# Tile 1's first h blocks, batch 1's second transposes and second x, and tile 1's PSUM banks placed anew in a fused attention and snake-MLP kernel

## The chip, the cores and the metric

The kernel runs on one core of one Trainium2 chip. Its time is device microseconds of one execution. Engines: PE (TensorE, matmuls), PEld (its weight loads), DVE (VectorE), ACT (ScalarE), POOL (GpSimd), SP (SyncE, which issues most DMAs).

## What is computed

Linear attention over 8 batches of 8 heads, 576 positions, 64 wide, then an MLP of width 512 -> 2048 -> 512 with a snake activation:

```python
def _attn_ref(q, k, v):
    q_s = exp(q - max(q, -1));  q_s = q_s / (sum(q_s, -1) + 1e-09)     # over the head's width
    k_s = exp(k - max(k, 2));   k_s = k_s / (sum(k_s, 2) + 1e-09)      # over the positions
    kv = np.einsum('bhsd,bhse->bhde', k_s, v)
    return np.einsum('bhsd,bhde->bhse', q_s, kv)

def _moe_ref(x, w_in, w_out, alpha):       # x: (4608, 512), the heads side by side
    h = x @ w_in
    s = np.sin(alpha * h)
    g = h + s * s / (alpha + 1e-09)
    return g @ w_out
```

## The kernel before

The 4608 positions make 8 batches for the attention and 9 tiles of 512 columns (`MF`) for the MLP. The program is a manual schedule: each engine runs its instructions in the order in which the Python code issues them, and waits at semaphores. So a line moved in the source moves work on every engine that it issues to.

Per batch, with the heads as two groups `ii` (0 and 1) of two pairs:

- `exp_half`, `exp_to` (L117): ACT takes exponentials of q and k, from fp32 stages filled by SP's DMAs, to bf16 `qe` and `ke`.
- `q1_sums`, `q1_norm` (L485 to L490): DVE sums and normalises q to `qn` for batch 1.
- `transpose_q1` (L472, with L199): eight PE transposes of one group into a PSUM tile `tp` of pool "a", copied by DVE to `qT` (L475).
- `cast_v1` (L467 to L470): v of batch 1 is cast to bf16 `vb`, places 0 to 4 of nine by ACT, 5 to 8 by POOL.
- `kv_mm` (L172): 36 small matmuls per group make k^T v, with the sums of k in one more column, in the PSUM tile `kvp` of pool `ps_k` (one buffer of two banks). `kv_norm` (L182, L183): DVE divides, to `kbd`.
- `x_half` (L477 to L481): `attn_x` (L216) multiplies `kbd` and `qT` in four matmuls into two banks; one bank is copied by ACT, the other by DVE, to two of the four 128-row chunks of `xT`, the MLP's input.

Per tile, with 16 blocks `ni` of 128 hidden units:

- `mm_h` (L254 to L262): four matmuls per block over the four chunks of `xT`, in the order `KO = (0, 2, 1, 3)`; chunks 0 and 2 come from group 0, 1 and 3 from group 1. `mm_h(t, ni, k0, k1)` does a part of the four; `h_slot` (L410) finishes a block that was begun.
- `sine` (L267): ACT's sine of the block, into one of four buffers `s`; the square is made by ACT (L269), POOL (L271) or DVE (L273), as the string `SQ` says for each block.
- `combine` (L277): DVE adds s*s/alpha and h, to `g`. With that the block's PSUM bank is free.
- `mm_o` (L281): 64 matmuls per tile of `g` with `w_out`; `evac_o` (L293, L296) copies the sums out and issues two output DMAs each on SP. `take(os, n)` issues the next n of a tile's `mm_o`.

PSUM has eight banks. In this stretch pools "a" and "b" have two each, "l" two, "k" (`ps_k`) two as one buffer. `BANKS` gives, for each tile, the pool of each of the 16 blocks; a pool hands out its buffers in turn, and the matmul that opens a buffer waits for the last reader of what lay there.

The change lies between tile 0's h blocks and tile 1's. There the code interleaves: the 64 `mm_o` of tile 0 (42, 10, 4, 4 and the last 4); batch 1's attention; then tile 1's 16 blocks. The parts stand in this order: norm and transposes of group 0; first kv (group 0); transposes of group 1; the loads of q's last place (`q8`) and of batch 2; cast of v's second group; first x; second kv; second x; exponentials of `q8`, and the sine table load (L525); tile 1's blocks (L554 to L557). `late_q8` uses `ps_k` again behind blocks 11 and 15. Then tile 1's `mm_o` start in the pools "o" and "p" (L561 on).

`load` and the `q8` loads are gated: a copy of one zero element by DVE (L514) stands ahead of a DMA into the same buffer, so that the DMA waits for it.

Of the kernel before, what the change touches and what calls it, by code (L numbers as in the profile page):

```python
# [15 lines left out]
F32 = mybir.dt.float32  # L16
# [7 lines left out]
def kernel(  # L24
# [23 lines left out]
    MF = 512  # L48
# [19 lines left out]
    xT = singles.tile([128, 4, NX], BF16, name="xT")  # L68
# [9 lines left out]
    def src_view(t, b):  # L78
        return t[b].rearrange("(i e) (p j) d -> (e p) i (j d)", e=2, j=J)
# [7 lines left out]
    def load(name, t, b, halves=False, eng=nc.sync, gate=None):  # L87

        st = stage.tile([128, 4, J, D], F32, name=f"st_{name}", tag="st")
        for ii in range(2) if gate else ():  # L90
            gate(st[:, ii, 0, 0:1], zero)
        view = src_view(t, b)
        flat = st.rearrange("p i j d -> p i (j d)")
        if halves:
            for ii in range(2):
                eng.dma_start(out=flat[:, ii::2], in_=view[:, ii::2])
        else:
            eng.dma_start(out=flat, in_=view)
        staged[name, b] = st

    def load_batch(b):
        load("q", q, b)
        load("k", k, b)
        load("v", v, b)
# [10 lines left out]
    def exp_to(dst, src, iis=range(2)):  # L115
        for ii in iis:
            nc.scalar.activation(dst[:, :, ii * 128:(ii + 1) * 128].rearrange("p j (x d) -> p x j d", x=2),  # L117
                                 src[:, ii::2], AX.Exp)
# [43 lines left out]
    def kv_mm(b, ii, pool, split=False):  # L162

        if ii == 0 or split:
            A["kvp", b] = pool.tile([128, 2, 512], F32, name="kvp", tag="a")
        kvp, ke, vt = A["kvp", b], A["ke", b], vb[b % 2]
        for j in range(J):
            for x in range(2):
                h = 2 * ii + x
                for e in range(2):  # L170
                    r = slice(64 * e, 64 * e + 64)
                    nc.tensor.matmul(kvp[64 * x:64 * x + 64, e, ii * 65:(ii + 1) * 65],  # L172
                                     ke[r, j, h * 64:(h + 1) * 64],
                                     vt[r, j, h * 65:(h + 1) * 65],
                                     start=(j == 0), stop=(j == J - 1))

    def kv_norm(b, i0=0, i1=2):

        kt, m = kbd[b % 2], i1 - i0
        kvr = small.tile([128, 2, 2], F32, name="kvr")[:, :, 0:m]  # L180
        src = A["kvp", b][:, :, i0 * 65:i1 * 65].rearrange("p e (ii c) -> p e ii c", ii=m)
        nc.vector.reciprocal(kvr, src[:, :, :, D])  # L182
        nc.vector.tensor_tensor(kt[:, :, i0:i1], src[:, :, :, 0:D],  # L183
                                kvr.unsqueeze(3).to_broadcast([128, 2, m, D]), op=ALU.mult)

    def q_tile(b):
        if ("qT", b) not in A:
            A["qT", b] = att2.tile([128, 2, J, 128], BF16, name="qT")
        return A["qT", b]
# [6 lines left out]
    def q_transpose_ii(b, ii, j0, j1, tp):  # L196

        for j in range(j0, j1):
            nc.tensor.transpose(tp[:, j - j0], A["qn", b][:, ii, j], identb)  # L199
# [11 lines left out]
    def attn_x(b, ii, j0, j1, outs):  # L211

        for e in range(2):
            for x in range(2):
                r = slice(64 * x, 64 * x + 64)
                nc.tensor.matmul(outs[x][64 * e:64 * e + 64], kbd[b % 2][r, e, ii],  # L216
                                 A["qT", b][r, ii, j0:j1, e * 64:(e + 1) * 64], start=True, stop=True)
# [24 lines left out]
    G = {}  # L242

    HP = {}
    BANKS = {0: "aabbkllaabbkllaa", 1: "kbbllaakbbllaabb", 2: "aabbopaabbopaabb"}

    def bank(kind):

        if kind == "k":
            return ps_k.tile([128, 2, MF], F32, name="kvp", tag="a")[:, 0]  # L250
        pool = {"a": lambda: ps_h[0], "b": lambda: ps_h[1], "l": lambda: ps_l, "o": lambda: ps_o[0], "p": lambda: ps_o[1]}[kind]()
        return pool.tile([128, MF], F32, name={"l": "lp", "o": "op", "p": "op"}.get(kind, "hp"), tag=kind)

    def mm_h(t, ni, k0=0, k1=4):  # L254

        if ni == 0 and k0 == 0:
            G[t] = gpool.tile([128, nN, MF], BF16, name="g")
        hp = HP[t, ni] if k0 else bank(BANKS.get(t, 3 * "aabb" + "abba")[ni])
        HP[t, ni] = hp
        for k in range(k0, k1):  # L260
            nc.tensor.matmul(hp, win[:, KO[k], ni * 128:(ni + 1) * 128],  # L261
                             xT[:, KO[k], t * MF % NX:t * MF % NX + MF], start=(k == 0), stop=(k == 3))  # L262
        return hp

    def sine(t, ni, hp, sq):
        s = spool.tile([128, MF], F32, name="s")
        nc.scalar.activation(s, hp, AX.Sin, scale=alpha_sb[:, ni:ni + 1])  # L267
        if sq == "A":
            nc.scalar.activation(s, s, AX.Square)  # L269
        elif sq == "P":  # L270
            nc.gpsimd.tensor_tensor(s, s, s, op=ALU.mult)  # L271
        else:
            nc.vector.tensor_tensor(s, s, s, op=ALU.mult)  # L273
        return s
# [25 lines left out]
    ACT_CP, DVE_CP, GP_CP = nc.scalar.copy, nc.vector.tensor_copy, nc.gpsimd.tensor_copy  # L300
# [21 lines left out]
    ps_k = ES.enter_context(tc.tile_pool(name="ps_k", bufs=1, space=PSUM, reuse_waits="tile"))  # L322
# [70 lines left out]
    xp = [bank("b") for _ in range(2)]  # L393
# [8 lines left out]
    xp = [bank("l") for _ in range(2)]  # L402
# [5 lines left out]
        mm_h(0, ni, ki, ki + 1)  # L408

    def h_slot(t, ni, sq, lag):  # L410
        hp = mm_h(t, ni, 2 if ni < (4, 1, 0)[min(t, 2)] else 0)
        lag.append((t, ni, hp, sine(t, ni, hp, sq)))

    def flush(lag, keep):
# [3 lines left out]
    def o_quad(t, accs, engs):  # L418

        R = range(4)  # L420
        by_m, by_n = [(n, m) for m in R for n in R], [(n, m) for n in R for m in R]
        orders = [by_m, by_n, by_n, by_n[:8] + [(n, m) for m in R for n in (2, 3)]]
        for c in R:
            for n, m in orders[c]:
                mm_o(t, m, 4 * c + n, accs[m])
                if c == 3 and n == 3:
                    evac_o(t, m, accs[m], engs[m])
                yield

    def take(it, n=1000):  # L430
        for _ in range(n):
            if next(it, 0) == 0:
                return
# [4 lines left out]
    with ES:  # L438
# [26 lines left out]
        os = o_quad(0, accs, [DVE_CP, ACT_CP, DVE_CP, DVE_CP])  # L465

        def cast_v1(ii):  # L467
            vv = vb[1].rearrange("p j (i c) -> p i j c", i=4)
            for j0, j1, eng in ((0, 5, ACT_CP), (5, 9, GP_CP)):
                eng(vv[:, 2 * ii:2 * ii + 2, j0:j1, 0:D], staged["v", 1][:, ii::2, j0:j1])  # L470

        def transpose_q1(ii, eng):  # L472
            tp = ps_h[0].tile([128, 8, 128], BF16, name="tp", tag="a")
            q_transpose_ii(1, ii, 0, 8, tp)
            eng(q_tile(1)[:, ii, 0:8], tp)  # L475

        def x_half(ii):  # L477
            xp = [bank("a") for _ in range(2)]
            attn_x(1, ii, 0, 8, xp)
            for x in range(2):  # L480
                (ACT_CP, DVE_CP)[x](xT[:, 2 * x + ii, MF:2 * MF], xp[x])  # L481

        def q1_sums(ii):
            part, src = qs1[:, :, 2 * ii:2 * ii + 2], qe1[:, ii]
# [3 lines left out]
        def q1_norm(ii):  # L488
            part = qs1[:, :, 2 * ii:2 * ii + 2]
            nc.vector.tensor_tensor(A["qn", 1][:, ii, 0:8].rearrange("p j (x d) -> p j x d", x=2), qe1[:, ii],  # L490
                                    part.unsqueeze(3).to_broadcast([128, 8, 2, D]), op=ALU.mult)
# [15 lines left out]
        exp_half("k", 1, 1)  # L507
        q1_norm(1)
        take(os, 10)
        kv_mm(1, 0, ps_k, split=True)  # L510
        kv_norm(1, 0, 1)
        transpose_q1(1, DVE_CP)
        for b in range(2):
            DVE_CP(q8[:, 0, b, 0:1], zero)  # L514
            nc.sync.dma_start(out=q8[:, :, b], in_=src_view(q, b)[:, :, 8 * D:J * D])
        load_batch(2)
        cast_v1(1)
        take(os, 4)
        x_half(0)
        kv_mm(1, 1, ps_k, split=True)  # L520
        kv_norm(1, 1, 2)
        take(os, 4)
        x_half(1)
        exp_to(A["qe", 1][:, J - 2:J], q8)
        nc.scalar.activation(zero, zero, AX.Sin)  # L525
        take(os)
        for ki in range(2):
            mm_h(1, 0, ki, ki + 1)
        norm_q8()
        load("q", q, 3)  # L530
        load("k", k, 3)
# [33 lines left out]
    def o_stream(t, eng=DVE_CP):  # L565
        for j in range(4):
            acc = bank("op"[j % 2])
            for ni in range(nN):
                mm_o(t, j, ni, acc)
                if ni == nN - 1:  # L570
                    evac_o(t, j, acc, eng)
                yield
# [4 lines left out]
    os = o_stream(1)  # L577
# [14 lines left out]
    for ii in range(2):  # L592
        xp = [bank("ab"[ii]) for _ in range(2)]
# [29 lines left out]
    for ni in range(nN):  # L623
# [4 lines left out]
        elif ni in (9, 13):  # L628
            ii = ni // 12
# [3 lines left out]
    for t in range(3, nT):  # L633
        b = t + 1 if t + 1 < B else None
        os = o_stream(t - 1)
# [9 lines left out]
        for ni in range(nN):  # L645
            hp = mm_h(t, ni)
# [62 lines left out]
```

## Time and profile before

| | |
|---|---|
| median of 3 runs | 283.23 us (282.95 to 283.6) |
| the profiled execution | 282.79 us, of it 281.0 us span of the profile |
| PE busy | 267.7 us (95%), 1890 matmuls |
| ACT busy | 223.8 us (80%) |
| DVE busy | 185.5 us (66%) |
| POOL busy | 81.3 us (29%) |
| granted PE clock | 9 tenths or more in every slice |
| DMA | 45.82 MB, mean 163 GB/s |

The span is what the profile sees, from the first instruction to the last. A time line shows start and length in us from the span's start, the engine, the line of the kernel, the operation, what it writes and reads, its shape, and in brackets the idle time of the engine just ahead of it with what ended that. Lengths overlap where an engine pipelines: matmuls above all, whose modelled end lies some 0.16 us behind the next one's start. The chain of waits follows the work that ended last back to what released it at each step. Some matmul records are missing from a trace, so a group of four can read x3.

### The profile page before, as it was taken

The page shows a single profiled execution, that of the slowest core. Times are in us where ns is not written, and L with a number is a line of the kernel's source. Part 1 is how long each engine was busy: PE and PEld are TensorE (multiplying, and loading weights), DVE is VectorE, ACT ScalarE, POOL GpSimd, SP SyncE. Part 2 cuts the span into 40 slices and gives each one's busy share as a digit, 9 for nine tenths or more (in the row PEclk, how much of TensorE's full clock was granted, in tenths as well). Part 3 has the DMA queues.
Part 4 walks back from the last instruction along what each step waited for, and adds up shares of the span by engine and source line. Part 5 has one row for each costly group of instructions (what it writes and reads, how often), then busy time and mean ns, then how long its engine had stood idle before and what let it go on. Part 6 is the DMA issues. An engine that isn't in the chain of part 4 may idle for free.

```text
span 281.0 us, 4925 instructions
## 1 busy us (share of the span) xinstructions
PE 267.7 (95%) x1890; PEld 124.0 (44%) x1919; DVE 185.5 (66%) x279; ACT 223.8 (80%) x322; POOL 81.3 (29%) x77
## 2 busy tenths in 40 slices
PE   2899989999999999999999999999999999999994
PEld 1444444444443444444444444444444444444443
DVE  3968776899878767766776677577775555555412
ACT  5899458999588999899989998999877777777400
POOL 2968121777667460205003500350000000000000
PEclk9999999999999999999999999999999999999999
DMA  7999999997599039712991199125011111111143
GB/s 263 299 194 232 278 307 319 361 343 253 120 229 399 2 81 334 290 37 48 267 383 45 37 263 392 38 50 124 8 29 40 37 37 37 40 41 42 40 106 75
DMA packets 39320, 45.82 MB, mean 163 GB/s; under 512 B 17008, under 2 KB 22656, under 8 KB 39296
## 3 DMA queue, kind: packets, MB, share of 16 engines
q1 hardware_dynamic: 33392, 40.58, 46.9%
q0 software_dynamic: 5744, 4.79, 10.3%
q8 instruction: 15, 0.25, 0.3%
q10 hardware_dynamic: 160, 0.13, 0.2%
q14 instruction: 9, 0.07, 0.1%
HBM read 36.71 MB, written 9.44 MB: 164 GB/s over the span
## 4 chain that ended last, share of the span: by engine, by line
PE 85%; DMA 8%; POOL 2%; issue 1%; SPq 1%; ACT 1%; DVE 1%; ACTq 0%
PE op L281 38%; PE hp L261 38%; DMA st_v<-in_v_dram 4%; DMA win<-in_moe_w_in_dram 2%; PE lp L261 2%; PE kvp L172 2%; DMA st_k<-in_k_dram 2%; PE op L261 1%; PE op L679 1%; POOL s L271 1%; PE kvp L261 1%; PE hp L216 1%; PE xp L216 1%; POOL st_v L306 1%; DVE g L277 1%
## 5 line engine op out<-in xcount | busy, mean ns | idle before, releaser
L277 DVE SCALAR_TENSOR_TENSOR g<-s,inva_sb,hp 128x512 bf16<-128x512 f32 x128 | 94.5, 746 | 58.7 <-ACT s L269 53.3
L261 PE MATMUL hp<-xT,win 128*128 128x512 bf16 x506 | 127.7, 379 | 0.6 <-PE lp L216 0.2
L281 PE MATMUL op<-wout,g 128*128 128x512 bf16 x478 | 121.0, 379 | 1.6 <-issue 1.1
L267 ACT ACTIVATE s<-hp,alpha_sb 128x512 f32<-128x512 f32 x128 | 86.1, 682 | 22.3 <-PE hp L261 21.0
L261 PEld LDWEIGHTS <-win 128*128 128x128 bf16 x576 | 55.7, 98 | 67.8 <-DMA win<-in_moe_w_in_dram 1.2
L281 PEld LDWEIGHTS <-g 128*128 128x128 bf16 x560 | 53.4, 98 | 64.8 <-issue 2.3
L269 ACT ACTIVATE s<-s 128x512 f32<-128x512 f32 x112 | 70.5, 630 | 3.5
L271 POOL TENSOR_TENSOR s<-s 128x512 f32<-128x512 f32 x29 | 30.1, 1053 | 17.6 <-ACT s L267 11.3
L151 POOL TENSOR_TENSOR qn<-qe,qs 128x1152 bf16<-128x1152 bf16 x11 | 23.2, 2127 | 29.5 <-DVE qs L145 24.4
L293 DVE COPY o<-op 128x512 f32<-128x512 f32 (+2 forms) x33 | 21.8, 661 | 10.2 <-PE op L281 7.9
L136 POOL CAST vb<-st_v 128x1152 bf16<-128x1152 f32 x12 | 14.7, 1257 | 45.6 <-DMA st_v<-in_v_dram 45.6
L117 ACT ACTIVATE qe<-st_q 128x1152 bf16<-128x1152 f32 (+2 forms) x18 | 17.7, 1025 | 6.1 <-DMA st_q<-in_q_dram 6.0
L117 ACT ACTIVATE ke<-st_k 128x1152 bf16<-128x1152 f32 x16 | 17.9, 1151 | 3.2 <-DMA st_k<-in_k_dram 3.2
L144 DVE TENSOR_REDUCE qs<-qe 128x36 f32<-128x2304 bf16 x5 | 12.8, 2551 | 8.3 <-ACT qe L117 8.3
L117 ACT ACT_TABLE_LOAD x7 | 9.0, 1283 | 0.8 <-PEq L693 0.7
L172 PE MATMUL kvp<-vb,ke 64*64 64x65 bf16 x576 | 6.9, 194 | 2.2 <-ACT vb L470 1.5
L349 PE MATMUL warm<-qe,identb 128*128 128x512 bf16 x10 | 4.1, 554 | 5.0 <-ACT qe L117 5.0
L281 PE MATMUL hp<-wout,g 128*128 128x512 bf16 x31 | 8.6, 379 | 0.1
L172 PEld LDWEIGHTS <-ke 64*64 64x64 bf16 x576 | 6.0, 106 | 6.1 <-issue 3.4
L281 PE MATMUL lp<-wout,g 128*128 128x512 bf16 x30 | 8.4, 379 | 0.2 <-issue 0.2
L261 PE MATMUL lp<-xT,win 128*128 128x512 bf16 x30 | 7.5, 379 | 0.1
L229 DVE CAST xT<-xp 128x1024 bf16<-128x1024 f32 (+1 forms) x7 | 7.4, 1065 | 0.0
(89 smaller groups left out, 135.8 us busy)
## 6 DMA issues: line engine op xcount, KB each, us to landing
out_dram<-o SPq DMA_DIRECT2D x70, 128.0 KB, 2.4
st_q<-in_q_dram SPq DMA_DIRECT2D x6, 1152.0 KB, 6.3
st_k<-in_k_dram SPq DMA_DIRECT2D x6, 1152.0 KB, 8.6
st_v<-in_v_dram SPq DMA_DIRECT2D x6, 1152.0 KB, 11.3
st_k<-in_k_dram SPq DMA_DIRECT2D x4, 576.0 KB, 8.1
st_q<-in_q_dram SPq DMA_DIRECT2D x4, 512.0 KB, 6.0
st_v<-in_v_dram SPq DMA_DIRECT2D x3, 576.0 KB, 10.0
wout<-in_moe_w_out_dram POOLq DMA_DIRECT2D x3, 512.0 KB, 12.7
```

The lines of the kernel that those rows point to most:

```text
L117: nc.scalar.activation(dst[:, :, ii * 128:(ii + 1) * 128].rearrange("p j (x d) -> p x j d", x=2), src[:, ii::2], AX.Exp)
L136: engs[ii](vv[:, 2 * ii:2 * ii + 2, :, 0:D], staged["v", b][:, ii::2])
L144: nc.vector.tensor_reduce(qs, A["qe", b].rearrange("p j (i d) -> p j i d", i=4), axis=AXL.X, op=ALU.add)
L151: engs[ii % len(engs)].tensor_tensor(qn[:, ii, 0:j1].rearrange("p j (x d) -> p j x d", x=2), qe[:, ii], part.unsqueeze(3).to_broadcast([12 ...
L172: nc.tensor.matmul(kvp[64 * x:64 * x + 64, e, ii * 65:(ii + 1) * 65], ke[r, j, h * 64:(h + 1) * 64], vt[r, j, h * 65:(h + 1) * 65], start= ...
L261: nc.tensor.matmul(hp, win[:, KO[k], ni * 128:(ni + 1) * 128], xT[:, KO[k], t * MF % NX:t * MF % NX + MF], start=(k == 0), stop=(k == 3))
L267: nc.scalar.activation(s, hp, AX.Sin, scale=alpha_sb[:, ni:ni + 1])
L269: nc.scalar.activation(s, s, AX.Square)
L271: nc.gpsimd.tensor_tensor(s, s, s, op=ALU.mult)
L277: nc.vector.scalar_tensor_tensor(G[t][:, ni], in0=s, scalar=inva_sb[:, ni:ni + 1], in1=hp, op0=ALU.mult, op1=ALU.add)
L281: nc.tensor.matmul(acc, G[t][:, ni, j * 128:(j + 1) * 128], wout[:, ni, :], start=(ni == 0), stop=(ni == nN - 1))
L293: eng(o[:, cols], acc)
```

## The change

- `BANKS[1]` is "aabbllkaabblaabb" in place of "kbbllaakbbllaabb".
- `h_slot` of tile 1 finishes two begun blocks (0 and 1), where it was one (0).
- `transpose_q1(1)` stands ahead of `kv_mm(1, 0)` and `kv_norm`, where it stood behind them.
- `cast_v1(1)`: the places 0 to 4 are cast by DVE, where it was ACT; it stands behind the first x, where it stood ahead of it.
- `x_half` takes its banks as an argument, and for group 0 ACT and DVE change places in the copies. Group 1's two banks are one tile of `ps_k`.
- The first two of the four matmuls of tile 1's blocks 0 and 1 stand between the first x and the second kv. Before, those of block 0 alone stood behind the last `mm_o` of tile 0.

```diff
-    BANKS = {0: "aabbkllaabbkllaa", 1: "kbbllaakbbllaabb", 2: "aabbopaabbopaabb"}
+    BANKS = {0: "aabbkllaabbkllaa", 1: "aabbllkaabblaabb", 2: "aabbopaabbopaabb"}
...
-        hp = mm_h(t, ni, 2 if ni < (4, 1, 0)[min(t, 2)] else 0)
+        hp = mm_h(t, ni, 2 if ni < (4, 2, 0)[min(t, 2)] else 0)
...
-            for j0, j1, eng in ((0, 5, ACT_CP), (5, 9, GP_CP)):
+            for j0, j1, eng in ((0, 5, (ACT_CP, DVE_CP)[ii]), (5, 9, GP_CP)):
...
-        def x_half(ii):
-            xp = [bank("a") for _ in range(2)]
+        def x_half(ii, xp):
             attn_x(1, ii, 0, 8, xp)
             for x in range(2):
-                (ACT_CP, DVE_CP)[x](xT[:, 2 * x + ii, MF:2 * MF], xp[x])
+                (ACT_CP, DVE_CP)[x ^ 1 ^ ii](xT[:, 2 * x + ii, MF:2 * MF], xp[x])
...
         take(os, 10)
+        transpose_q1(1, DVE_CP)
         kv_mm(1, 0, ps_k, split=True)
         kv_norm(1, 0, 1)
-        transpose_q1(1, DVE_CP)
...
         load_batch(2)
+        take(os, 4)
+        x_half(0, [bank("a") for _ in range(2)])
         cast_v1(1)
-        take(os, 4)
-        x_half(0)
+        for ki in range(2):
+            for ni in range(2):
+                mm_h(1, ni, ki, ki + 1)
         kv_mm(1, 1, ps_k, split=True)
         kv_norm(1, 1, 2)
         take(os, 4)
-        x_half(1)
+        xb = ps_k.tile([128, 2, MF], F32, name="kvp", tag="a")
+        x_half(1, [xb[:, x] for x in range(2)])
...
         take(os)
-        for ki in range(2):
-            mm_h(1, 0, ki, ki + 1)
```

## The prediction

> **What bounds the kernel now.** I read the page first (PE busy 95% of the span, granted clock full in every slice), then the waits of PE: after 59 us it waits for no other engine to the end of the span (1.1 us of "issue" in seven pieces is all that is listed). So whatever moves the moment at which tile 1's out matmuls (L281, first at 59.7 us) begin, moves the end by the same amount; only the stretch from 36 to 60 us has to be worked out. The chain of waits there:
>
> ```profile
> 29.41 12.43 DMA st_v<-in_v_dram
> 41.86 0.75 ACT vb L470
> 42.65 0.48 PE kvp L172 x32
> 43.13 1.00 PE hp L281 x4
> ...
> 45.44 0.86 PE kvp L261 x4
> ```
>
> Batch 1's second half of v lands at 41.84, ACT casts it, and only then PE's second kv product runs; from there the chain is PE alone. PE's time line (start, length, instruction, idle time before it):
>
> ```profile
> 41.00 0.41 PE L216 MATMUL hp<-qT,kbd 64*64 64x512 bf16 x4
> 42.65 0.48 PE L172 MATMUL kvp<-vb,ke 64*64 64x65 bf16 x36 [1.24 <-ACT vb L470]
> 43.11 1.02 PE L281 MATMUL hp<-wout,g 128*128 128x512 bf16 x4
> 44.06 0.41 PE L216 MATMUL hp<-qT,kbd 64*64 64x512 bf16 x4
> 44.63 0.81 PE L281 MATMUL lp<-wout,g 128*128 128x512 bf16 x3 [0.16 <-issue]
> 45.28 1.03 PE L261 MATMUL kvp<-xT,win 128*128 128x512 bf16 x4
> ...
> 55.92 3.62 PE L261 MATMUL hp<-xT,win 128*128 128x512 bf16 x16
> ```
>
> The hole of 1.24 us ahead of the second kv is all there is to gain. Blocks 12 to 15 of tile 1 are the last row. A 128x512 matmul takes a slot of 0.216 us (L261's rows: 45.28 to 46.14 for four). ACT:
>
> ```profile
> 40.49 1.16 ACT L117 ACTIVATE ke<-st_k 128x1152 bf16<-128x1152 f32 x1 [1.36 <-DMA st_k<-in_k_dram]
> 41.86 0.74 ACT L470 CAST vb<-st_v 128x640 bf16<-128x640 f32 x1 [0.21 <-DMA st_v<-in_v_dram]
> 42.50 0.57 ACT L481 CAST xT<-hp 128x512 bf16<-128x512 f32 x1
> 44.17 0.58 ACT L293 COPY o<-hp 128x512 f32<-128x512 f32 x1 [1.10 <-PE hp L281]
> 44.65 0.59 ACT L481 CAST xT<-hp 128x512 bf16<-128x512 f32 x1
> 47.29 0.67 ACT L267 ACTIVATE s<-kvp,alpha_sb 128x512 f32<-128x512 f32 x1
> ```
>
> After its last copy of x, ACT has a fixed road to tile 1's first sine: from 44.65 to 47.29, 2.64 us (two exponentials, a table load). From 47.29 to 56.5 ACT never waits for PE. DVE at the end of that stretch:
>
> ```profile
> 55.84 0.75 DVE L277 SCALAR_TENSOR_TENSOR g<-s,inva_sb,hp 128x512 bf16<-128x512 f32 x1 [0.20 <-POOL s L271]
> 56.51 0.85 DVE L273 TENSOR_TENSOR s<-s 128x512 f32<-128x512 f32 x1
> 57.27 0.73 DVE L277 SCALAR_TENSOR_TENSOR g<-s,inva_sb,hp 128x512 bf16<-128x512 f32 x1
> ```
>
> These are block 8's combine, the square of block 10, block 9's combine: a PSUM bank comes free when its combine ends, block 8's at 56.59, block 9's at 58.01.
>
> **The change, part by part.** Clock times are those of the profiled run, so shifts can be read off.
>
> *Transposes ahead of the first kv (L199, L172).* PE is free at 38.80 (last L281 starts at 38.58), DVE's second norm ends at 38.67. Eight transposes take 0.44 (39.59 to about 40.04 before), kv follows at about 39.33 (0.09 for the change of tile size, as in the profile between L281 and L216) and ends at 39.8, 0.15 later than before. DVE now copies the transposes ahead of the norm of kv: 39.44 to 40.13, then 0.17 + 0.29 to about 40.55. The four L281 end at 40.61, the first x (L216) starts at 40.70 instead of 41.00. Worth 0.3 us to the copies of x, but ACT is busy with ke until 41.65 either way.
>
> *v's cast moved from ACT to DVE (L470), copies of x swapped.* ACT loses 0.74 us and its wait for v: its copy of x runs 41.55 to 42.13 instead of 42.50 to 43.07. DVE's copy of x runs 41.19 to 41.88, then the cast. The trace has the same shape on DVE once, in the start: 128x640, 0.62 us. With POOL casting its share at that moment (41.89, 0.62) the far bound is the trace's worst stretch of a POOL square, 1.49 beside a median near 1.04: 0.72 x 1.43 = 1.03, so v is ready between 42.5 and 42.95. I take 42.6; PE needs it at 43.13, so the cast costs nothing, with 0.2 us of cover even at the far bound.
>
> [...]
>
> *Blocks 0 and 1 begun behind the first x (L261).* Two mm_h of two k each, four matmuls, wait for ACT's copy: 42.18 to 43.04. Before, only two such (block 0) ran, later. The second kv starts at 43.04 + 0.09 = 43.13 instead of 42.65: **+0.48**. Everything behind it follows in the old order and spacing (kv to the first L261: 45.28 - 42.65 = 2.63): the second x at 44.54, ACT's evacuation (L293) and last copy of x +0.48, the remaining L261 from 45.76. There 60 of 64 matmuls are left; before, 60 were left at 46.14. So PE alone would be **0.38 ahead**.
>
> *Second x in kv's banks.* Both halves now lie in one tile, and in the changed kernel as built DVE's copy of the second half waits for ACT's copy of the first, which was not so before (DVE's began at 44.55, ACT's at 44.65, side by side). ACT's ends at 45.24 + 0.48 = 45.72, DVE's (0.69, L481) runs to 46.45, and block 0's last k waits until 46.50. Behind DVE's copy stand two evacuations and q8's norm, which ends near 49.2, before the first combine at 49.6. Before, the sixth L261 began at 45.28 + 5 x 0.216 = 46.36: PE is now **0.14 behind**.
>
> *Banks rotated.* Blocks 12 to 15 now take the banks of blocks 7 to 10 (distance 5). Before, the distances there were 7, 7, 6, 6. Block 14 waited for block 8's combine (56.59) and began at 55.92 + 8 x 0.216 = 57.65. Now it waits for block 9's, 58.01 in the old run: 0.41 us late (with 0.05 for the semaphore) even if ACT were not late at all. But the sines start 0.48 later (47.77), and since ACT runs without a wait for PE from there, every combine up to block 9 shifts by the same 0.48. Block 12 waits until 55.64 + 0.53 = 56.17 (0.10 behind PE's own 56.06), block 13 until 57.12, block 14 until 58.01 + 0.53 = 58.54: **+0.89**. Block 15 (block 10's combine, 58.67 + 0.48) is free in time. PE's 0.14 is inside that stall, not added to it. The out matmuls then follow 0.89 late; the last combine (62.89, shifted some 0.5, by sine 15 at about 60.9) is ready before its matmul at 62.95 + 0.89.
>
> *Queues.* q8's two loads hang on two DVE copies of one element, now at 40.55 instead of 40.85. SP's next three loads (batch 2) follow 0.3 us earlier. Nobody waits for them before 45.1 (q8) and 62 (batch 2). At worst they take 0.3 us from v's landing, and 42.6 + 0.3 is still before 43.13. Two ACT casts less and one DVE cast more: no other engine waits for these.
>
> **Sum.** PE is +0.48 at the second kv, -0.38 where the L261 resume, +0.14 at block 0's end, +0.89 from block 14 on. After that PE has no stall in which to lose it. The profiled run took 282.79 (span 281.0 and 1.8 around it), so its counterpart would take 283.68. The median of the runs is 283.23, so I predict 283.23 + 0.89 = **284.1 us**; by the bounds of the switch before the second kv (0 or 0.09) and of the cast, 283.9 to 284.3.
>
> **Rivals.**
> B: the ring does not bind, only DVE's wait for ACT counts: +0.14, 283.4. It would need ACT's sines to catch up 0.75 us before block 9. Against it: ACT's only slack there is about 0.1 us (52.74 to 52.76 and the like).
> C, the other side: the hole is filled and nothing given back: -0.38, 282.85. Its place is the L261 resuming at 45.76; it decides if DVE's copy does not really wait for ACT's and combine 9 ends before 57.3, that is 0.7 us earlier than in the old run. For it: ACT sheds 0.74 us. Against: that is shed ahead of the x copy, and spent again waiting for the later kv.
> D: more is lost. If the profiled run's v landed early, or casts and squares slow each other like the 1.49 us POOL row, combine 9 slips by another 0.45: +1.3, 284.5.
> The reverse also weakens the forecast: where v lands later in other runs, before pays for it and after does not, until 0.5 us; with 0.3 of that the loss is 0.6.
>
> **Numbers.** Chances: forecast 0.62, B 0.13, C 0.12, D 0.13. About 0.2% (0.57 us) is what a measurement tells from no change: the forecast and D are beyond it but for the case of a late v (0.04); B and most of C are within; a part of C, with luck in the runs, is beyond on the fast side. So slower 0.71, same 0.20, faster 0.09. The range reaches from between C and B to above D: 283.0 to 284.7.
>
> **What would show it.** In the new profile: the first x near 40.7; four L261 near 42.2 with the hole gone; the second kv near 43.1; DVE's copy from kvp starting as ACT's ends, near 45.75, with PE idle about half a us; the first sine near 47.8; PE idle ahead of block 14, released by DVE L277, the out matmuls at 60.6. Wrong if the first sine starts before 47.3 or the copies run side by side.

## The result, and the profile after

| | before | after |
|---|---|---|
| median of 22 runs each | 282.61 us (281.86 to 284.51) | 283.87 us (283.61 to 285.43) |
| the profiled execution | 282.79 us, span 281.0 | 283.86 us, span 282.1 |
| second kv (L172) starts | 42.65 | 43.15 |
| tile 1's first sine (L267) starts | 47.29 | 47.75 |
| block 14 (L261) starts | 57.65 (worked out: 55.92 + 8 x 0.216) | 58.74 |
| first out matmul (L281) starts | 59.71 | 60.81 |

The ratio is 1.0043, with a 95% interval of 1.0032 to 1.0053: the change makes the kernel slower by 1.26 us. The two profiled executions differ by 1.07 us, and the first out matmul by 1.10. From 59 us on PE waits for no other engine; all that is listed there is "issue", 1.1 us in seven pieces, as before:

```profile
PE op L281 <- issue: 1.1, 7, 0.2
PE hp L261 <- DVE g L277: 0.4, 1, 0.4
```

(Waits of PE in the kernel after, from 59 us to the end: total, times, longest, in us. The second line is the wait that ended at 58.74, ahead of the row that reaches into this stretch.) So the loss lies whole between 40 and 61 us. PE's time line there (start, length, instruction, idle time before it):

```profile
40.98 0.41 PE L216 MATMUL hp<-qT,kbd 64*64 64x512 bf16 x4
42.18 1.04 PE L261 MATMUL hp<-xT,win 128*128 128x512 bf16 x4 [0.79 <-DVE xT L480]
43.15 0.48 PE L172 MATMUL kvp<-vb,ke 64*64 64x65 bf16 x36
45.76 0.38 PE L261 MATMUL hp<-xT,win 128*128 128x512 bf16 x1
46.49 2.53 PE L261 MATMUL hp<-xT,win 128*128 128x512 bf16 x11 [0.35 <-DVE xT L480]
...
56.16 2.18 PE L261 MATMUL hp<-xT,win 128*128 128x512 bf16 x8
58.74 1.89 PE L261 MATMUL hp<-xT,win 128*128 128x512 bf16 x8 [0.40 <-DVE g L277]
```

The hole of 1.24 us that the kernel before had ahead of the second kv is gone. In its place stand 0.79 ahead of the four early matmuls, 0.35 inside block 0, 0.40 ahead of block 14, and one that no bracket shows: blocks 12 and 13 (56.16) take 2.18 where eight matmuls take 1.89, so 0.29 is idle ahead of block 13. Starts with the same work left tell it best: against the kernel before, PE is 46.49 - 46.36 = 0.13 behind at the sixth L261, 56.16 - 55.92 = 0.24 at block 12, 1.09 at block 14. Nearly all of the loss arises in the last stretch of the tile.

ACT, DVE and POOL show why. ACT:

```profile
44.63 0.59 ACT L293 COPY o<-hp 128x512 f32<-128x512 f32 x1 [2.58 <-PE hp L281]
45.12 0.59 ACT L480 CAST xT<-kvp 128x512 bf16<-128x512 f32 x1
47.75 1.25 ACT L267 ACTIVATE s<-hp,alpha_sb 128x512 f32<-128x512 f32 x2
...
50.96 1.35 ACT L267 ACTIVATE s<-lp,alpha_sb 128x512 f32<-128x512 f32 x2
```

DVE (four of its rows; L158 and L159, a reduction and a reciprocal of q8's norm, end just ahead of L160):

```profile
42.04 0.71 DVE L470 CAST vb<-st_v 128x640 bf16<-128x640 f32 x1
45.74 0.69 DVE L480 CAST xT<-kvp 128x512 bf16<-128x512 f32 x1 [0.85 <-ACT xT L480]
48.49 0.69 DVE L160 TENSOR_TENSOR qe<-qe,qs 128x512 bf16<-128x512 bf16 x1
50.12 2.06 DVE L277 SCALAR_TENSOR_TENSOR g<-s,inva_sb,hp 128x512 bf16<-128x512 f32 x3 [0.93 <-POOL s L271]
```

ACT idles 2.58 us, because what it copies out (L293) hangs on the later kv; its copy of x starts at 45.12, DVE's only as that ends. POOL:

```profile
41.78 0.62 POOL L470 CAST vb<-st_v 128x512 bf16<-128x512 f32 x1 [2.38 <-DMA st_v<-in_v_dram]
48.51 1.58 POOL L271 TENSOR_TENSOR s<-s 128x512 f32<-128x512 f32 x1 [6.10 <-DVE qs L159]
```

The first square of the tile takes 1.58 us, where the same instruction took 1.03 in the kernel before:

```profile
48.04 1.03 POOL L271 TENSOR_TENSOR s<-s 128x512 f32<-128x512 f32 x1 [5.53 <-DVE qe L160]
```

In the kernel after it starts 0.02 us behind DVE's product L160 and ends at 50.09; the first combine follows at 50.12. From there, by the code and the times, the delay goes on over the four buffers `s`: sine 4 writes the buffer that block 0's combine has to have read. That combine ends at 50.12 + 0.75 = 50.87, and sine 4 starts at 50.96 (the profile names no releaser for so short a wait), 3.21 behind the first sine. (In the kernel with q8's norm moved ahead, told below, it is 2.95.) Every later sine, square and combine stands behind that.

The chain of waits ahead of block 14 leads through four instructions:

```profile
55.44 1.05 POOL s L271
56.49 0.03 issue
56.52 0.75 DVE g L277
57.27 0.76 DVE s L273
58.03 0.67 DVE g L277
58.70 0.04 issue
```

Block 8's square, block 8's combine, block 10's square, block 9's combine: then block 9's bank is free, and block 14 opens it. That is the ring of banks with its new distance of 5. Block 9's combine starts at 57.95, where it started at 57.27 before. Of these 0.68 us, 0.46 is the later first sine, and 0.22 was added behind it.

### The profile page after: what moved, and what is told of

Its sections match the earlier page's. It is cut to its first block, busy times and chain, and to the rows that moved or that the text cites. A ratio compares the mean times of both kernels' runs of the same rounds, so it can differ in the third digit from the quotient of the medians.

```text
span 282.1 us, 4926 instructions
## 1 busy us (share of the span) xinstructions
PE 268.0 (95%) x1890; PEld 123.8 (44%) x1919; DVE 186.1 (66%) x280; ACT 223.7 (79%) x321; POOL 82.0 (29%) x77
## 4 chain that ended last, share of the span: by engine, by line
PE 88%; DMA 5%; POOL 2%; issue 1%; DVE 1%; ACT 1%; SPq 0%; ACTq 0%
PE op L281 38%; PE hp L261 37%; DMA win<-in_moe_w_in_dram 3%; PE hp L281 3%; PE lp L281 2%; PE kvp L172 2%; DMA st_k<-in_k_dram 2%; PE lp L261 2%; PE op L261 1%; PE op L680 1%; POOL win L107 1%; PE hp L216 1%; ACT s L267 1%; PE xp L216 1%; PE kvp L261 1%
## 5 line engine op out<-in xcount | busy, mean ns | idle before, releaser
L277 DVE SCALAR_TENSOR_TENSOR g<-s,inva_sb,hp 128x512 bf16<-128x512 f32 x130 | 95.8, 745 | 59.7 <-ACT s L269 53.3
L261 PE MATMUL hp<-xT,win 128*128 128x512 bf16 x514 | 129.7, 379 | 2.2 <-DVE xT L480 1.1
L281 PE MATMUL op<-wout,g 128*128 128x512 bf16 x478 | 121.0, 379 | 1.6 <-issue 1.1
L267 ACT ACTIVATE s<-hp,alpha_sb 128x512 f32<-128x512 f32 x130 | 87.5, 684 | 22.3 <-PE hp L261 20.6
L261 PEld LDWEIGHTS <-win 128*128 128x128 bf16 x576 | 55.8, 98 | 70.3 <-issue 2.4
L281 PEld LDWEIGHTS <-g 128*128 128x128 bf16 x560 | 53.4, 98 | 64.6 <-issue 2.1
L271 POOL TENSOR_TENSOR s<-s 128x512 f32<-128x512 f32 x29 | 30.7, 1073 | 18.2 <-ACT s L267 12.1
L293 DVE COPY o<-op 128x512 f32<-128x512 f32 (+2 forms) x33 | 21.8, 660 | 10.5 <-PE op L281 8.3
L281 PE MATMUL hp<-wout,g 128*128 128x512 bf16 x30 | 8.6, 379 | 0.3 <-issue 0.2
L281 PE MATMUL lp<-wout,g 128*128 128x512 bf16 x31 | 8.7, 379 | 0.0
L172 PEld LDWEIGHTS <-ke 64*64 64x64 bf16 x576 | 5.8, 106 | 4.8 <-issue 2.6
L172 PE MATMUL kvp<-vb,ke 64*64 64x65 bf16 x576 | 6.9, 194 | 1.0 <-ACT vb L331 0.6
L229 DVE CAST xT<-xp 128x1024 bf16<-128x1024 f32 (+1 forms) x7 | 7.4, 1065 | 0.0
L261 PE MATMUL lp<-xT,win 128*128 128x512 bf16 x26 | 6.8, 379 | 0.4 <-DMA win<-in_moe_w_in_dram 0.3
```

The costliest lines, as they stand in the source:

```text
L277: nc.vector.scalar_tensor_tensor(G[t][:, ni], in0=s, scalar=inva_sb[:, ni:ni + 1], in1=hp, op0=ALU.mult, op1=ALU.add)
L281: nc.tensor.matmul(acc, G[t][:, ni, j * 128:(j + 1) * 128], wout[:, ni, :], start=(ni == 0), stop=(ni == nN - 1))
L293: eng(o[:, cols], acc)
```

## The experiments

In all of them "before" is the kernel before, run on the same chip in the same comparison; times are medians. A stretch is read as the same two marks in each trace: "kv to out" is from the second kv's start to the first out matmul (17.06 us before, 17.66 after). Starts with a star are worked out from a longer row with 0.216 us a matmul.

| kernel | second kv | first sine | block 14 | first out | time minus before |
|---|---|---|---|---|---|
| before | 42.65 | 47.29 | 57.65* | 59.71 | |
| after | 43.15 | 47.75 | 58.74 | 60.81 | +1.26 |
| ring widened in after | 43.06 | 47.67 | 57.78* | 60.30 | +0.71 |
| new ring in before | 42.39 | 47.00 | 57.78 | 59.85 | +0.31 |
| no early blocks | 42.94 | 47.54 | 58.52 | 60.59 | +0.88 |
| q8's norm earlier | 43.28 | 47.88 | 58.65 | 60.72 | +1.15 |
| one copy on DVE | 43.22 | 47.33 | 58.20 | 60.27 | +0.85 |

**The ring alone, both ways.** In the kernel after, the last blocks get banks with longer distances; block 14 takes block 8's again (distance 6), as before the change:

```diff
-    BANKS = {... 1: "aabbllkaabblaabb", ...}
+    BANKS = {... 1: "aabbllkaabllbaab", ...}
```

> The changed kernel with tile 1's banks as aabbllkaabllbaab: blocks 12 to 15 reuse the banks of blocks 3, 7, 8, 9 (distances 9, 6, 6, 6) instead of 7, 8, 9, 10 (all 5). Ring theory: block 14 waits for block 8's combine (57.3 in the changed kernel's trace) and not block 9's (58.6), so PE's 0.40 us of idle ahead of block 14 goes; the first out matmul moves from 60.8 to about 60.4, where it now waits for block 11's combine (its bank is the one of block 11), so some 0.4 us less than the changed kernel, +0.8 over before. Rival, the DVE copy's wait for ACT is the loss: nothing changes, +1.2 over before.

Measured: 283.33 against 282.62, ratio 1.0029 (1.0019 to 1.0040). PE (two rows of its time line):

```profile
56.05 3.63 PE L261 MATMUL hp<-xT,win 128*128 128x512 bf16 x16
60.30 1.89 PE L281 MATMUL op<-wout,g 128*128 128x512 bf16 x8 [0.34 <-DVE g L277]
```

Blocks 12 to 15 run through without a stall. Almost half of the loss is gone (+0.71 in place of +1.26), though a new wait of 0.34 stands ahead of the out matmuls: it ends with block 11's combine, since the bank that the first of them opens was now block 11's. The reverse, the new string in the kernel before and nothing else:

```diff
-    BANKS = {... 1: "kbbllaakbbllaabb", ...}
+    BANKS = {... 1: "aabbllkaabblaabb", ...}
```

> The kernel before with nothing but the changed bank string of tile 1. Ring theory: block 14 waits for block 9's combine, 58.01 in the trace of before, and starts at 58.06 instead of 57.65: +0.41 us over before, PE idle just ahead of block 14, released by the combine. Rival, the rotation is harmless by itself: 0.0.

Measured: 282.93 against 282.62, ratio 1.0008 (0.9995 to 1.0020). By time alone this is no difference that the runs can tell; the trace shows the mechanism all the same:

```profile
55.59 1.89 PE L261 MATMUL hp<-xT,win 128*128 128x512 bf16 x8
57.78 1.89 PE L261 MATMUL hp<-xT,win 128*128 128x512 bf16 x8 [0.30 <-DVE g L277]
```

Block 14 could start at 55.59 + 8 x 0.216 = 57.32 and starts at 57.78. So the ring costs 0.46 us with the old timing of the sines, where 0.41 was reckoned. In both kernels with the new string block 14 waits for block 9's combine (0.30 and 0.40).

**The early blocks.** The four early matmuls go back behind the last out matmuls:

```diff
-        for ki in range(2):
-            for ni in range(2):
-                mm_h(1, ni, ki, ki + 1)
         kv_mm(1, 1, ps_k, split=True)
...
         take(os)
+        for ki in range(2):
+            for ni in range(2):
+                mm_h(1, ni, ki, ki + 1)
         norm_q8()
```

> The changed kernel with the four early matmuls of blocks 0 and 1 put back behind the last matmuls of tile 0's output, all else as changed. Theory (ACT's late start, handed on by the ring, sets the end): the second kv starts when DVE's cast of v is done, about 42.8 instead of 43.15, ACT's first sine at 47.4 instead of 47.75, block 14 and the end 0.35 us earlier than in the changed kernel, +0.85 over before, although PE loses the four matmuls in the hole. Rival, PE's own order is the bound (filling the hole is worth 0.86 less the 0.35 of the earlier kv): 0.5 us slower than the changed kernel, +1.7 over before.

Measured: 283.50 against 282.62, ratio 1.0035 (1.0020 to 1.0049).

```profile
42.94 0.48 PE L172 MATMUL kvp<-vb,ke 64*64 64x65 bf16 x36 [1.50 <-DVE vb L470]
...
58.52 1.89 PE L261 MATMUL hp<-xT,win 128*128 128x512 bf16 x8 [0.40 <-DVE g L277]
```

The kv comes only 0.21 earlier, not 0.48, because now v's cast on DVE holds it. Block 14 still waits 0.40, and it comes as much earlier (0.22) as the sines (0.21). So the end follows ACT and the ring, not the amount of work that PE has done ahead: the early blocks' lead, 0.38 by the prediction, is worth nothing here.

**DVE's wait for ACT.** The two banks of the second x are copied by DVE in one instruction, which takes the copy off ACT:

```diff
-        x_half(1, [xb[:, x] for x in range(2)])
+        attn_x(1, 1, 0, 8, [xb[:, x] for x in range(2)])
+        DVE_CP(xT[:, 1::2, MF:2 * MF], xb)
```

> The changed kernel with both halves of the second x copied by one DVE instruction (1.07 us, as the 128x1024 casts elsewhere), so DVE does not wait for ACT, and ACT is rid of its copy. Theory (ACT's first sine, handed on by the ring, sets the end): ACT's road starts 0.47 us earlier, first sine near 47.3, and block 14 starts 10.8 to 11.0 behind it as in the changed kernel and in the two runs with its ring (47.75 to 58.74; 47.54 to 58.52; 47.00 to 57.78): near 58.1 to 58.25, the end 0.5 to 0.65 earlier, +0.6 to +0.75 over before. Rival, PE's own order sets it: block 0's last k at 46.3 instead of 46.5, the end 0.2 earlier, +1.0 over before.

Measured: 283.44 against 282.59, ratio 1.0027 (1.0015 to 1.0038). The copy takes 1.23 us (not 1.07: the 128x1024 casts elsewhere in these traces, L229, take 1.22 too), almost as long as the two in a row (1.31, 45.12 to 46.43), so PE waits as before (0.36). But the first sine starts at 47.33. That is 0.42 of the 0.54 gained at block 14 and at the out matmuls; the other 0.12 arises behind the first sine, and there POOL's first square took 1.04 in place of 1.58 in this kernel (its row stands below). This kernel keeps the new ring: an earlier sine and a wider ring each take about half a us off the first out matmul, by two ways to the same stall.

**The slow square.** q8's norm goes ahead of DVE's two evacuations, so that its product is done before POOL's square:

```diff
-        take(os)
         norm_q8()
+        take(os)
```

> The changed kernel with q8's norm issued on DVE ahead of the two evacuations of tile 0's last sums instead of behind them. In the changed kernel's trace POOL's first square of tile 1 took 1.58 us (48.51 to 50.09) beside DVE's product of that norm (48.49 to 49.18), against 1.04 for the other squares. Theory (these two block each other, and 0.2 us of it reaches PE): the norm ends near 48.0, the square takes 1.04, the first combine comes at 49.6 instead of 50.1, sine 4 no longer waits, and the end is 0.2 us earlier than in the changed kernel: +1.0 over before. Rival, ACT and the ring alone set it: the first combine moves, the end does not.

Measured: 283.77 against 282.62, ratio 1.0043 (1.0031 to 1.0055). The time can't tell; the trace can. POOL and ACT:

```profile
48.63 1.03 POOL L271 TENSOR_TENSOR s<-s 128x512 f32<-128x512 f32 x1 [6.43 <-ACT s L267]
```

```profile
50.83 1.26 ACT L267 ACTIVATE s<-lp,alpha_sb 128x512 f32<-128x512 f32 x2
```

The square takes 1.03 again, sine 4 starts 50.83 - 47.88 = 2.95 behind the first sine, and from the first sine to block 14 it is 58.65 - 47.88 = 10.77, in place of 10.99: 0.22 less. The new ring in the kernel before, where the product also lies ahead of the square, has 10.78. In the kernel with one copy on DVE the order was the other one. DVE and POOL:

```profile
48.34 1.33 DVE L160 TENSOR_TENSOR qe<-qe,qs 128x512 bf16<-128x512 bf16 x1
```

```profile
48.09 1.04 POOL L271 TENSOR_TENSOR s<-s 128x512 f32<-128x512 f32 x1 [5.87 <-DVE qs L158]
```

Here POOL came first and kept its 1.04, and DVE's product grew from 0.69 to 1.33. The later one ends 0.91 (POOL) and 0.54 (DVE) behind the earlier, most of its own 1.03 and 0.69, and the earlier is not slowed (0.69 and 1.04): in these two pairs one waits and the other pays nothing.

**Can the good parts be had without the costs?** Three tries. First, one early block in place of two, two separate banks for the second x, and a ring to fit:

```diff
-    BANKS = {... 1: "aabbllkaabblaabb", ...}
+    BANKS = {... 1: "abbllakabbllaabb", ...}
-        hp = mm_h(t, ni, 2 if ni < (4, 2, 0)[min(t, 2)] else 0)
+        hp = mm_h(t, ni, 2 if ni < (4, 1, 0)[min(t, 2)] else 0)
-            for ni in range(2):
-                mm_h(1, ni, ki, ki + 1)
+            mm_h(1, 0, ki, ki + 1)
-        xb = ps_k.tile([128, 2, MF], F32, name="kvp", tag="a")
-        x_half(1, [xb[:, x] for x in range(2)])
+        x_half(1, [bank("a"), bank("k")])
```

> The changed kernel with block 0 alone begun ahead of the second kv (two matmuls instead of four), the second x in two separate tiles (one of pool a, one of kv's banks) so that ACT and DVE copy side by side, and banks abbllakabbllaabb (distances 7, 6, 6, 6 at blocks 12 to 15). Theory: the second kv waits for DVE's cast of v, about 42.9; 0.43 us of matmuls are already done, nothing is serial behind it and block 14 does not wait: 0.1 to 0.2 us either side of the kernel before. Rival, begun blocks cost something by themselves: over +0.5.

Measured: 282.75 against 282.59, ratio 1.0008 (0.9995 to 1.0021). With two tiles the copies run side by side (DVE 44.74, ACT 44.84), though nothing else about them is changed: so the wait came with the shared tile, not with the engines. What is left is v's cast, which holds the kv at 42.87, and a wait of 0.34 ahead of the out matmuls. DVE and POOL:

```profile
41.87 0.95 DVE L470 CAST vb<-st_v 128x640 bf16<-128x640 f32 x1
```

```profile
41.84 0.62 POOL L470 CAST vb<-st_v 128x512 bf16<-128x512 f32 x1 [2.54 <-DMA st_v<-in_v_dram]
```

Then the same with v's second cast in three parts, so that DVE's is shorter (DVE places 0 to 2, ACT 3 and 4, POOL 5 to 8):

```diff
-            for j0, j1, eng in ((0, 5, (ACT_CP, DVE_CP)[ii]), (5, 9, GP_CP)):
+            for j0, j1, eng in (((0, 5, ACT_CP), (5, 9, GP_CP)), ((0, 3, DVE_CP), (3, 5, ACT_CP), (5, 9, GP_CP)))[ii]:
```

> As e6_two_early_parallel, with v's second cast in three parts: places 0 to 2 DVE, 3 and 4 ACT (idle at that time), 5 to 8 POOL. Theory: v is ready near 42.5, the second kv starts when the two early matmuls end, near 42.7, no later than in the kernel before by more than 0.1 to 0.3, and 0.43 us of matmuls are done: 0.1 to 0.4 us faster than before. Rival, the casts hold each other up on DVE and POOL: kv near 43, no gain.

Measured: 282.75 against 282.59, ratio 1.0009 (0.9998 to 1.0021): nothing gained. In the profiled execution PE itself was late (the kv at 43.06), and 0.34 us of wait stood ahead of the out matmuls. Last, on top of that, tile 1's out matmuls begin with pool "p" in place of "o", so that they need not wait for that bank:

```diff
-            acc = bank("op"[j % 2])
+            acc = bank("po" [j % 2] if t == 1 else "op"[j % 2])
```

> As e6v_and_v_cast_split, but tile 1's out matmuls take their two banks in the other order, so that the first does not wait for block 11's combine (0.34 us of idle PE in e6v_and_v_cast_split and e6_two_early_parallel). Theory: from the second kv to the first out matmul 16.7 us instead of 17.03 (17.06 in the trace of before), the end 0.2 to 0.3 earlier than in e6v_and_v_cast_split: 282.5, some 0.1 below the kernel before, not to be told from it. Rival, the last combine now comes too late and PE waits there instead: no gain over e6v_and_v_cast_split.

Measured: 282.70 against 282.50, ratio 1.0017 (1.0006 to 1.0029).

```profile
42.51 0.48 PE L172 MATMUL kvp<-vb,ke 64*64 64x65 bf16 x36
...
59.13 2.12 PE L281 MATMUL op<-wout,g 128*128 128x512 bf16 x9
...
62.77 0.39 PE L281 MATMUL op<-wout,g 128*128 128x512 bf16 x1 [0.23 <-DVE g L277]
```

From kv to out it takes 16.62 us, 0.44 less than before. PE then arrives before block 15's combine and waits 0.23 at the last of the first 16 out matmuls. In its profile this leaves 0.2 us (span 280.8 against 281.0). But that profile is of the fastest of its 11 runs (282.55), and the one of before of a run above the median (282.79), so the 0.2 is no gain: by the medians this kernel is 0.20 slower, and its interval lies above 1. Why the shorter way from kv to out doesn't show in the medians stays open. No kernel here beats the one before.

**All three costs undone in the kernel after,** with its early blocks kept: the wide ring, the one copy on DVE and the earlier norm, as in the diffs above.

> The changed kernel with its four early matmuls kept and three costs taken out together: the wide ring of e1_ring_wide, the one DVE copy of e2_one_dve_copy, q8's norm first as in e5_norm_q8_first. Theory: first sine near 47.3, L261 resumed near 46.1 with 60 matmuls left (46.14 in the trace of before), no wait at blocks 12 to 15: within 0.2 us of the kernel before, so 1.1 us less than the changed kernel. Rival, something of the change is not yet named: more than +0.4 over before stays.

Measured: 283.06 against 282.59, ratio 1.0015 (1.0002 to 1.0027): 0.8 of the 1.26 us comes back, and 0.47 stays, more than was expected: it is the rival of the expectation that fits, something not yet named. Its profiled execution (284.31) was its slowest run, with everything later by more than 1 us from its loads on, so only distances can be read in it: kv to out is 16.63. So nothing is lost behind the kv any more (17.06 before), and what remains should lie ahead of it: the kv now follows the first x, its copies and four matmuls, where it followed v alone (43.06 to 43.28 in the four profiles with four early matmuls that are in the table, 42.39 and 42.65 without the change). Any lateness of PE, which before vanished in the hole of 1.24 us, is now paid. That is an argument from the traces, and it covers the 0.47 only in part: these kv are 0.41 to 0.89 later, and 0.43 of that is won back behind the kv, which leaves between nothing and 0.46. The run meant to show it settled nothing. It is the same kernel with the early blocks moved back:

> As e7_all_three_undone, but with the four early matmuls put back behind tile 0's last output matmuls: what the early start is worth once the ring, the serial copies and the locked square are gone. Theory: the second kv starts 0.2 to 0.35 earlier (DVE's cast of v sets it), the way from there to tile 1's first out matmul is 0.86 longer, less the 0.36 that PE waits for the one DVE copy in e7_all_three_undone: the end is 0.15 to 0.3 later than there, so some +0.6 to +0.8 over before. Rival, the early start is worth nothing: equal or earlier than e7_all_three_undone.

Measured: 283.18 against 282.50, ratio 1.0012 (1.0003 to 1.0021), but in two groups: five runs from 282.53 to 282.71, six from 283.18 to 284.39. The median of such a set says little. The profile is of the slowest of them; what it shows is told at the end.

## Why the prediction was right, and where it was off

- **Transposes ahead, first x at 40.70:** 40.98. In that execution PE was about 0.26 late from its start on; the copies and the early matmuls (42.18) came at the predicted time, since ACT set them, as the prediction said.
- **Early blocks, kv +0.48:** 43.15, +0.50. Right in size, but not all of it is theirs: without them the kv came at 42.94, held by v's cast. Of the 0.50, 0.21 goes away with the early blocks.
- **v's cast on DVE, ready at 42.6:** it ended at 42.75, with no cost in this kernel, but how long it takes hangs on POOL's share. DVE's cast took 0.48 us where POOL's ended 0.10 after its start (one copy on DVE), 0.71 where they overlapped by 0.36 (42.04 and 42.40), and 0.95 where they began together (two separate banks): it ends some 0.35 us after POOL's each time. The row from which the prediction took its far bound (1.49 beside 1.04) shows a wait of the same kind, in the kernel before: POOL's square (56.76, 1.49) began 0.25 behind DVE's square of block 10 (56.51, 0.85) and ended 0.89 behind it. (The far bound, 0.72 x 1.43, also takes 0.72 where the row it names has 0.62.) The range's upper end, 284.3, allows for a cost of the cast that no run of this kernel shows: DVE's cast ended at 42.75, and PE came at 43.15. Where the early blocks are fewer or gone, the cast holds the kv (42.87 and 42.94).
- **Second x in one tile:** DVE's copy behind ACT's at 45.74 (45.72 predicted), block 0's last k at 46.49 (46.50), the first sine at 47.75 (47.77).
- **Ring:** block 14 at 58.74, predicted 58.54. This is the term that was mis-sized: +1.09 in place of +0.89. The step that failed is "q8's norm, which ends near 49.2, before the first combine at 49.6", and with it "every combine up to block 9 shifts by the same 0.48". The norm did end at 49.18, but POOL's square began 0.02 us behind the start of its product, took 1.58 in place of 1.03, and ended at 50.09 in place of some 49.55. The first combine came at 50.12, sine 4 had to wait for its buffer, and block 9's combine shifted by 0.68. The sum had weighed DVE and POOL in each other's way for the casts alone and not for the product.
- **From block 14 on:** +1.10 at the out matmuls, 1.07 in the profiled times. "PE has no stall in which to lose it" held.
- **The sum:** 284.1 was predicted and 283.87 came, but two errors cancel there. The three runs of before shown first had a median of 283.23, the 22 here (these three among them) 282.61, which is 0.62 less. The difference was 1.26 in place of 0.89. So that the time came within 0.25 us of the forecast is luck; that the kernel is slower, and where, is not. Of the 0.37, some 0.2 is the square, and 0.18 is that the profiled execution of before (282.79) lay that much above its median, while that of after lay on its own.

The rivals: B (the ring does not bind) and C (a gain of 0.38) fell; PE waits 0.40 for block 9's combine, which ended at 58.70, not before 57.3. D (squares slow each other, +0.45) had a slowed square right, at half the size and one only. That a late v would be paid for by before alone wasn't tried; the runs of after do lie closer together (all but one from 283.61 to 284.24).

## What to carry to other kernels

A wait that an engine sits out ahead of a stage is worth filling only if that stage's end hangs on it: here a ring of banks and the sines' start set the end, so 0.38 us of matmuls done early bought nothing, and starting the sines 0.46 us late cost about as much as the ring itself. Before one shortens the distance in a ring of buffers, one should work out from the trace when the reader of each bank ends; a distance cut from 6 or 7 to 5 cost 0.46 by itself at block 14, in the trace (the runs' times alone can't tell it). And where a pair that held each other up here (DVE's product or square beside POOL's square, DVE's cast beside POOL's) slides together, price the later of the two with the rest of the earlier one, at the place where the consumer waits: 1.58 in place of 1.03 for POOL's square put 0.22 us on the way to block 14.

## What the runs showed of the hardware that was not expected

**The clock fell behind one short hole.** In the kernel with all costs and the early blocks undone, PE idled 1.75 us ahead of the kv (41.02 to 42.77). PE's rows behind it, and the stretches of that execution (from : to, length; busy us of PE, PEld, DVE, ACT, POOL with counts; granted clock; DMA share; GB/s):

```profile
42.77 0.48 PE L172 MATMUL kvp<-vb,ke 64*64 64x65 bf16 x36 [1.75 <-DVE vb L470]
43.19 1.59 PE L281 MATMUL hp<-wout,g 128*128 128x512 bf16 x4
```

```profile
40.12:43.53 3.41, 1.66 (x45) 0.79 (x44) 2.16 (x7) 1.64 (x2) 0.62 (x1) 1.00 0.88 161
43.53:46.94 3.41, 3.08 (x11) 0.88 (x10) 2.51 (x4) 2.10 (x4) 0.00 (x0) 0.50 0.99 345
46.94:50.35 3.41, 3.41 (x17) 1.55 (x16) 2.37 (x5) 2.39 (x5) 1.03 (x1) 1.00 1.04 406
```

The half clock lasted for 3.41 us. In the 3.41 us ahead of it PE was busy for 1.66 (49%); under it four matmuls took 1.59 in place of 1.04. Kv to out was 18.57. The kernel without early blocks has a hole of nearly the same length, 1.50 us, and there the clock stayed full:

```profile
38.63:42.05 3.42, 2.65 (x54) 1.33 (x53) 2.16 (x7) 2.01 (x3) 1.12 (x2) 1.00 0.91 250
42.05:45.46 3.41, 2.36 (x47) 1.23 (x49) 1.90 (x5) 1.09 (x4) 0.39 (x1) 1.00 0.90 236
```

There the two stretches were busy to 78% and 69%. From 40.12 to 43.53, as in the rows of the half clock, it was 51% (1.75 of 3.41), with full clock behind it; in the kernel before, 62% (2.12 of 3.41), also with full clock behind it. The ends of two executions settle it no better: the kernel after was busy to 19% from 277.87 to 281.28 (0.64 of 3.41), and from there its clock was 0.50; in the kernel before PE had no work from 277.41 to the end of the span at 280.98, and the clock stayed full. So the length of the hole alone does not tell it (half clock behind 1.75 us, none in 3.57), and 49% and 51% are one execution each, with a single drop in midstream to go by. What sets it off is not shown.

This does not make the two groups of that kernel's runs. The mean granted clock on record for each run is 0.994 in the profiled one, which is what one such stretch costs (half of 3.41 of 282.6 us is 0.006); in the other five of the slower six it is 1.0. What parts the groups stays open. In the other runs whose clock is on record the mean is below 0.997 only once: 0.992, in the slowest run (285.09) of the kernel without early blocks, the only other one here with a hole of 1.5 us in its trace.

**In three pairs of DVE and POOL the one that came second was held up,** on either engine: 1.58 against 1.03 for POOL's square, 1.33 against 0.69 for DVE's product, 0.95 against 0.48 for DVE's cast. The first kept its time: 0.69 for the product, 1.04 for the square, 0.62 for POOL's cast. Not every pair does this: in the kernel before, DVE's combine (50.92, 0.75) ran inside a row of POOL's squares that took 4.03 for four.
